# RWKV attention and ELU feed-forward on one core: a new written order for the first part of block 0

## The chip, the core and the metric

The kernel runs on one core of a Trainium2 chip. A core has five engines that matter here: PE (TensorE, matmuls and transposes by matmul), DVE (VectorE), ACT (ScalarE), POOL (GpSimd) and SP (SyncE, which here only issues loads). Each executes its own list of instructions in order, and they wait for each other by semaphores. The metric is the device time of one execution in microseconds (us).

## What is computed

```python
state = 0                                   # per batch b, head h: 48 x 48
for t in range(768):                        # B=4, H=8, S=768, D=48
    y[t]  = r[t] @ (state + outer(u * k[t], v[t]))
    state = w[:, None] * state + outer(k[t], v[t])
x = y as 3072 tokens x 384
h = x @ w_in                                # 384 -> 2048
g = where(h > 0, h, exp(min(h, 0)) - 1)
out = g @ w_out                             # 2048 -> 384
```

## The kernel before

The sequence is cut into six blocks of 128 tokens, and a block holds all four batches, so 4 x 128 = 512 tokens go through the feed-forward at once. A *unit* is one block of one batch: its r and k are turned by PE (`turn_in`, L628), multiplied by tables of powers of w (L688), multiplied with each other (`scores`, L768), masked, and applied to v (`first_outputs`, L880 and L824). The result is split in two halves of lower precision, xh (L899 on ACT) and xl (L901 on DVE). A *step* f of the feed-forward, 0 to 15, is one slice of 128 hidden columns: `hidden` (9 matmuls, L1031), `negative` (two on ACT, L1040 and L1041), `elu` (DVE, L1046), `split_g` (gh on ACT, L1052; gl on DVE, L1054), `project` (9 matmuls, L1075). `hidden(f)` uses the weights wh and wl of index f, part 1, and `project(f)` those of index f + 1, part 0.

In block 0 the weights arrive too. Load `Lw:j` brings w_in of f = j/2 for even j (four transfers, L212) and w_out of f = (j-1)/2 for odd j (one, L215) into six staging slots. Pair k is made of the loads 2k-1 and 2k: `wd:k` (`widen`, ACT, L571) reads both, `ma:k` (`merge`, DVE, L580) joins them, `sp:k` (`split_w`, POOL L591 and ACT L593) makes wh, and `rs:j` or `rsd:j` (`rest_w`, POOL L615 or DVE L615 and L617) makes wl, which frees the slot. `rsd:6` makes the part of wl that `hidden(3)` reads, called wl_131 in the order listings.

What stands when is written out by hand. `START` lists everything up to the first half of step 0, `BOTH` the steps 0 to 2 mixed with what block 1 needs early (`nT`: turning r and k of unit (1, 0), after `Lnk:0` loaded them; `ndr`, `ndk`: their tables). Steps 3 to 15 follow the line `FIRST`, later blocks `LATER`. Each name calls one function, and its instructions are put at the end of the lists of the engines that it uses. A name's variants differ in the engine:

```python
"kr": lambda b: self.key_rest(0, b),          # POOL, L740
"krd": lambda b: self.key_rest(0, b, dve),    # DVE
"m0": lambda b: self.mask_scores(0, b, 0),          # DVE
"m0a": lambda b: self.mask_scores(0, b, 0, True),   # ACT, then POOL
"S": lambda b: self.new_state(0, b),          # PE L924, then ACT L941
"Sd": lambda b: self.new_state(0, b, dve),    # PE L924, then DVE L941
```

Of the kernel before, what the change touches and what calls it, by code (L numbers as in the profile page):

```python
# [20 lines left out]
B, H, S, D = 4, 8, 768, 48  # L21
# [17 lines left out]
DEEP, WIDE = 3, 2  # L39

START = """
Lrk:2 Lv:1 Lrk:3 Lv:2 Lw:0 Lv:3 Lw:2 Lw:1 Lw:4 Lw:3 Lw:5
pr jk:8 inv rua:0 Tr:0 ub rub:0 Tk:0 dr:0 Tr:1 PT dk:0 A:0 dr:1 sum:0 rua:1 krd:0 zw m0:0 rub:1 Tk:1 vd:0 m1:0 ru:2
S:0 dk:1 Tk:2 Tr:2 A:1 ru:3 dr:2 dk:2 m0:1 sum:1 m1:1 Tr:3 dr:3 Tk:3 vd:1 dk:3 A:2 sum:2 Y:0 m0:2 wd:0 vd:2 A:3 m1a:3
sum:3 m0:3 xh:0 wdi:1 m1:2 Y:1 vd:3 ma:0 sp:0 wdo:1 xl:0 Y:2 xh:1 xh:2 rsd:0 mai:1 Lw:6 krd:3 spi:1 xl:1 mao:1 Y:3 H:0
"""
BOTH = """
xh:3 xl:2 xl:3 hid0 rsd:2 krd:2 wd:2 neg0 krd:1 spo:1 hid1 ma:2 elu0 sp:2 gh0 rs:1 Lnk:0 rs:3 neg1 Lw:8 gl0 Sd:1 rsd:4
wd:3 Sd:2 elu1 Lw:7 Lw:9 S:3 Lw:10 gh1 ma:3 proj0 sp:3 hid2 nT:0 gl1 nru:0 neg2 wd:4 proj1 rsd:6 Lnv:1 elu2 nsum:0 gh2
ma:4 ndr:0 ndk:0 Lnv:0 gl2 sp:4 rsd:5 Lw:12 wd:5 rsd:8 Lw:11 Lnk:1 rsd:7 nDp:0  # L50
"""
FIRST = """
Lq rk3 v3 Eq1 hid ns3 A1 T0 rud0 ma sum0 bkA-1 neg df0 elu sp dk0 pa1 brA-1 Y2 gh gl dr0 pb1 r4d xh2 xl2 mbT+1 mrT+1
# [1104 lines left out]
```

## Time and profile before

| | us |
|---|---|
| median of 3 runs | 497.84 (497.4 to 498.88) |
| the profiled execution | 498.67 |
| its span, first to last instruction | 496.9 |
| PE busy in the span | 485.8 (98%) |
| DVE, ACT, POOL busy | 304.7, 240.7, 106.5 |
| first `hidden` matmul starts at | 25.14 |
| `hidden(3)` starts at | 38.55 |

Times in the profile count from the start of the span. The profiled execution is 1.77 us longer than its span. A timeline row gives start, duration, engine, line, operation, names, size, and in brackets the idle time of the engine before it with what ended it; rows of the same kind in sequence are merged.

### The profile page before, as it was taken

The numbers are of one execution on the slowest core, as the hardware profiler recorded it, in microseconds if no ns is written. First come the engines' busy times: TensorE is split into PE (matmuls) and PEld (weight loads), VectorE is DVE, ScalarE is ACT, GpSimd is POOL, SyncE is SP. The second block draws the span as 40 slices with busy tenths as digits, with TensorE's granted clock in tenths as the row PEclk, the third lists the DMA queues.
The fourth block names the chain that finished last, engine by engine and source line by source line (L and its number), as shares of the span: only waits on it lengthen the run. The fifth ranks groups of instructions, "written<-read, shape, count | busy, mean of one in ns | idle before, by whom it ended". The sixth has DMA issues, their size and how long they took to land.

```text
span 496.9 us, 12118 instructions
## 1 busy us (share of the span) xinstructions
PE 485.8 (98%) x5013; PEld 403.2 (81%) x5013; DVE 304.7 (61%) x533; ACT 240.7 (48%) x458; POOL 106.5 (21%) x142
## 2 busy tenths in 40 slices
PE   8999999999999999999999999999999999999995
PEld 6787778787788888888888888888888878899995
DVE  7889998884676556657456575564674343433332
ACT  4278766744354444535435435445354354444442
POOL 7623332432132321221321321301011000000000
PEclk9999999999999999999999999999999999999999
DMA  8999986483454642544613625514443000011001
GB/s 136 225 215 201 211 203 195 83 166 92 111 96 119 134 113 41 139 113 72 125 49 86 150 67 110 138 44 91 108 80 90 11 1 2 8 33 24 1 0 69
DMA packets 108453, 49.11 MB, mean 99 GB/s; under 512 B 89442, under 2 KB 104292, under 8 KB 108388
## 3 DMA queue, kind: packets, MB, share of 16 engines
q1 hardware_dynamic: 96292, 43.52, 40.1%
q10 hardware_dynamic: 12096, 4.72, 3.9%
q8 instruction: 41, 0.67, 0.6%
q14 instruction: 24, 0.20, 0.1%
HBM read 35.12 MB, written 13.11 MB: 97 GB/s over the span
## 4 chain that ended last, share of the span: by engine, by line
PE 85%; DMA 6%; SPq 4%; DVE 2%; ACT 1%; issue 1%; DVEq 0%; ACTq 0%
PE ps_acc L1075 38%; PE ps_h L1031 36%; PE ps_a L792 4%; DMA stage<-in_moe_w_out_dram 3%; PE ps_y L824 3%; SPq L212 2%; PE ps_y L812 1%; DMA stage<-in_moe_w_in_dram 1%; PE ps_y L924 1%; SPq L169 1%; PE ps_y L807 1%; DMA r_t<-in_r_dram 1%; SPq L165 1%; ACT wide L571 1%; PE ps_a L768 0%
## 5 line engine op out<-in xcount | busy, mean ns | idle before, releaser
L1031 PE MATMUL ps_h<-x,wh 128*128 128x512 f32 (+1 forms) x582 | 193.9, 388 | 1.4 <-ACT x L899 1.3
L1075 PE MATMUL ps_acc<-g,wh 128*128 128x512 f32 x480 | 164.5, 397 | 0.1
L1046 DVE SCALAR_TENSOR_TENSOR ps_h<-g,ps_h 128x512 f32<-128x512 f32 x96 | 66.6, 694 | 129.9 <-ACT g L1041 129.8
L1031 PEld LDWEIGHTS ps_h<-x,wh 128*128 128x128 f32 x582 | 108.8, 188 | 24.2 <-ACT x L899 1.5
L1040 ACT ACTIVATE g<-ps_h 128x512 f32<-128x512 f32 x96 | 57.3, 597 | 128.6 <-PE ps_h L1031 102.5
L1031 PE MATMUL ps_h<-x,wl 128*128 128x512 f32 (+1 forms) x291 | 112.8, 388 | 0.0
L1075 PEld LDWEIGHTS ps_acc<-g,wh 128*128 128x128 f32 x480 | 90.1, 188 | 21.1 <-issue 0.8
L1075 PE MATMUL ps_acc<-g,wl 128*128 128x512 f32 x240 | 93.7, 390 | 0.0
L1054 DVE SCALAR_TENSOR_TENSOR g<-ps_h,g 128x512 fp32r<-128x512 f32 x96 | 66.3, 690 | 40.1 <-ACT g L1052 35.9
L1052 ACT ACTIVATE g<-ps_h 128x512 fp32r<-128x512 f32 x96 | 57.4, 598 | 67.8 <-DVE ps_h L1046 67.6
L1031 PEld LDWEIGHTS ps_h<-x,wl 128*128 128x128 f32 x291 | 54.6, 188 | 10.8
L1041 ACT ACTIVATE g<-g 128x512 f32<-128x512 f32 x96 | 60.7, 632 | 3.1
L842 POOL TENSOR_TENSOR a<-ident,diag 128x512 f32<-128x512 f32 x20 | 20.9, 1043 | 151.5 <-PE ps_y L924 88.9
L1075 PEld LDWEIGHTS ps_acc<-g,wl 128*128 128x128 f32 x240 | 45.1, 188 | 8.5
L676 POOL TENSOR_TENSOR tb<-rk,qw 128x512 f32<-128x512 f32 x16 | 20.7, 1294 | 69.9 <-DMA rk<-blocks 62.1
L1075 PE MATMUL ps_acc<-wh,g 128*128 128x384 f32 x128 | 35.2, 338 | 0.1
L849 DVE COPY_PREDICATED a<-mask,ps_a 128x512 f32<-128x512 int32 x40 | 29.3, 731 | 0.0
L838 ACT ACTIVATE a<-ident,diag 128x128 f32<-128x128 f32 x80 | 25.3, 392 | 0.0
L1075 PEld LDWEIGHTS ps_acc<-wh,g 128*128 128x128 f32 x128 | 23.4, 188 | 1.2 <-issue 0.5
L571 ACT ACTIVATE wide<-stage 128x768 f16<-128x768 bf16 (+1 forms) x18 | 17.8, 991 | 12.5 <-DMA stage<-in_moe_w_in_dram 10.6
L949 ACT CAST x<-ps_y 128x256 fp32r<-128x256 f32 (+1 forms) x40 | 10.8, 324 | 23.1 <-DVE state L939 21.6
L1075 PE MATMUL ps_acc<-wl,g 128*128 128x384 f32 x64 | 21.5, 336 | 0.0
(114 smaller groups left out, 438.5 us busy)
## 6 DMA issues: line engine op xcount, KB each, us to landing
blocks<-tb SPq DMA_DIRECT2D x64, 128.0 KB, 2.3
rk<-blocks SPq DMA_DIRECT2D x16, 512.0 KB, 3.5
stage<-in_moe_w_out_dram SPq DMA_DIRECT2D x16, 383.8 KB, 5.8
stage<-in_moe_w_in_dram SPq DMA_DIRECT2D x64, 95.8 KB, 4.5
out_dram<-stage ACTq DMA_DIRECT2D x80, 48.0 KB, 1.7
r_t<-in_r_dram SPq DMA_DIRECT2D x17, 192.0 KB, 4.3
k_t<-in_k_dram SPq DMA_DIRECT2D x17, 192.0 KB, 5.0
v_t<-in_v_dram SPq DMA_DIRECT2D x17, 192.0 KB, 5.3
```

Of the source, the lines that this page charges most:

```text
L571: self.nc.scalar.activation(top.rearrange("p s (f t) -> p s f t", t=2)[..., 1], self.place(self.late, k, DEEP, i).bitcast(BF16)[..., 2], A ...
L676: (self.nc.gpsimd if i else self.nc.vector).tensor_mul(dst, src, by)
L838: self.nc.scalar.activation(un["a"][i][:, a, :], self.ident, AF.Copy, scale=diag[:, a : a + 1])
L842: self.nc.gpsimd.tensor_mul(un["a"][i], self.ident.unsqueeze(1).to_broadcast([P, HP, P]), diag.unsqueeze(2).to_broadcast([P, HP, P]),)
L849: self.nc.vector.copy_predicated(un["a"][i], self.mask.bitcast(I32).unsqueeze(1).to_broadcast([P, HP, P]), un["pa"][i].rearrange("p (a t) ...
L1031: self.nc.tensor.matmul(ph[:, part], lhsT=a[:, c * P : (c + 1) * P], rhs=x[:, c, part], start=(c == 0 and i == 0), stop=(c == NC - 1 and i ...
L1040: nc.scalar.activation(g, ph, AF.Relu, scale=-1.0)
L1041: nc.scalar.activation(g, g, AF.Exp, scale=-1.0)
L1046: self.nc.vector.scalar_tensor_tensor(ph, g, -1.0, ph, op0=ALU.add, op1=ALU.max)
L1052: nc.scalar.activation(part, g, AF.Copy, scale=W_SCALE)
L1054: nc.vector.scalar_tensor_tensor(part, g, W_SCALE, self.g[n, f][2].bitcast(F32), op0=ALU.mult, op1=ALU.subtract)
L1075: self.nc.tensor.matmul(at, lhsT=lhs, rhs=rhs, start=(f == 0 and i == 0), stop=(f == NF - 1 and i == 2),)
```

## The change

Two of the four tables are written anew, `START` and `BOTH`; `FIRST`, `LATER` and all functions stay. The set of work is the same, and so is the work of each engine but for the entries whose variant changes: key_rest of all four units goes from DVE to POOL (`krd` to `kr`), rest_w 5 and 7 too (`rsd` to `rs`), `vd:0` from POOL to DVE, the first masked scores of unit 0 from DVE to ACT and POOL (`m0a:0`) and those of unit 3 the other way (`m1:3`), the state copies of units 2 and 3 change places between DVE and ACT.

```diff
 START = """
-Lrk:2 Lv:1 Lrk:3 Lv:2 Lw:0 Lv:3 Lw:2 Lw:1 Lw:4 Lw:3 Lw:5
-pr jk:8 inv rua:0 Tr:0 ub rub:0 Tk:0 dr:0 Tr:1 PT dk:0 A:0 dr:1 sum:0 rua:1 krd:0 zw m0:0 rub:1 Tk:1 vd:0 m1:0 ru:2
-S:0 dk:1 Tk:2 Tr:2 A:1 ru:3 dr:2 dk:2 m0:1 sum:1 m1:1 Tr:3 dr:3 Tk:3 vd:1 dk:3 A:2 sum:2 Y:0 m0:2 wd:0 vd:2 A:3 m1a:3
-sum:3 m0:3 xh:0 wdi:1 m1:2 Y:1 vd:3 ma:0 sp:0 wdo:1 xl:0 Y:2 xh:1 xh:2 rsd:0 mai:1 Lw:6 krd:3 spi:1 xl:1 mao:1 Y:3 H:0
+rua:0 ub Lrk:3 jk:8 Tr:0 rub:0 pr rua:1 rub:1 Tk:0 inv Lrk:2 Tr:1 dr:0 Tk:1 Lw:0 dk:0 A:0 dr:1 m0a:0 dk:1 sum:0 PT
+Lv:1 m1:0 Lv:2 Tr:3 vdd:0 A:1 sum:1 zw dr:3 Tk:3 m1:1 Tr:2 Tk:2 m0:1 dr:2 Y:0 Lv:3 wd:0 dk:2 A:2 dk:3 ma:0 Lw:1 Lw:2
+xh:0 ru:3 sum:3 xl:0 kr:0 sp:0 wdo:1 Lw:4 m0:2 S:0 Lw:3 ru:2 sum:2 vd:1 m1:2 vd:2 rsd:0 A:3 Y:1 xh:1 m0:3 wdi:1 m1:3
+Y:2 mao:1 xh:2 vd:3 xl:1 kr:1 Lw:6 mai:1 xl:2 Y:3 H:0 xh:3 xl:3 spi:1 rsd:2 Lw:5 wd:2
 """
 BOTH = """
-xh:3 xl:2 xl:3 hid0 rsd:2 krd:2 wd:2 neg0 krd:1 spo:1 hid1 ma:2 elu0 sp:2 gh0 rs:1 Lnk:0 rs:3 neg1 Lw:8 gl0 Sd:1 rsd:4
-wd:3 Sd:2 elu1 Lw:7 Lw:9 S:3 Lw:10 gh1 ma:3 proj0 sp:3 hid2 nT:0 gl1 nru:0 neg2 wd:4 proj1 rsd:6 Lnv:1 elu2 nsum:0 gh2
-ma:4 ndr:0 ndk:0 Lnv:0 gl2 sp:4 rsd:5 Lw:12 wd:5 rsd:8 Lw:11 Lnk:1 rsd:7 nDp:0
+Sd:1 hid0 neg0 ma:2 spo:1 kr:3 elu0 wd:3 gh0 Sd:3 Lnk:0 rs:1 hid1 sp:2 kr:2 neg1 gl0 ma:3 S:2 Lw:8 nT:0 rsd:4 Lw:7
+elu1 proj0 sp:3 Lnk:1 gh1 rs:5 Lw:11 Lw:10 hid2 nru:0 gl1 rs:3 proj1 nsum:0 nDp:0 wd:4 Lw:9 ma:4 neg2 sp:4 ndr:0 Lnv:0
+rs:7 elu2 rsd:8 gh2 ndk:0 wd:5 gl2 rsd:6 Lnv:1 Lw:12
 """
```

**First place: DVE, the end of `BOTH`.** These are DVE's instructions from `rsd:6` (the row that writes wl_131 by L617) to the last of step 2 in the kernel before; L1046 is `elu2`, L1054 is `gl2`, L580 is `ma:4`, the L688 rows are `ndr` and `ndk`.

```order
L617 SCALAR_TENSOR_TENSOR wl_131<-stage,wh_130 128x384
L1046 SCALAR_TENSOR_TENSOR ps_h<-g,ps_h 128x512
L733 TENSOR_REDUCE diag<-ru 128x8
L580 SCALAR_TENSOR_TENSOR stage<-stage,wide 128x768
L688 TENSOR_TENSOR rk<-ps_rT,pw 128x512
L688 TENSOR_TENSOR rk<-ps_kT,qw 128x512
L1054 SCALAR_TENSOR_TENSOR g_728<-ps_h,g_721 128x512
L615 TENSOR_TENSOR wl_131<-stage,wh_130 128x384
L617 SCALAR_TENSOR_TENSOR wl_133<-stage,wh_132 128x384
```

And DVE at the same place in the changed kernel, from `ma:4` on:

```order
L580 SCALAR_TENSOR_TENSOR stage<-stage,wide 128x768
L688 TENSOR_TENSOR rk<-ps_rT,pw 128x512
L1046 SCALAR_TENSOR_TENSOR ps_h<-g,ps_h 128x512
L617 SCALAR_TENSOR_TENSOR wl_133<-stage,wh_132 128x384
L688 TENSOR_TENSOR rk<-ps_kT,qw 128x512
L1054 SCALAR_TENSOR_TENSOR g_737<-ps_h,g_733 128x512
L617 SCALAR_TENSOR_TENSOR wl_131<-stage,wh_130 128x384
```

The L617 that writes wl_131 moved from ahead of `elu2` to behind `gl2`, and L617 of wl_133 (`rsd:8`) stands between `elu2` and `ndk`. On PE nothing changed there: `hidden(3)` follows `project(1)`, and its second matmul reads wl_131.

**Second place: PE, between `hidden(1)` and `project(0)`.** Before, after the last matmul of `hidden(1)`, come the products for the new states of units 1 to 3 (L924):

```order
L1031 MATMUL ps_h<-x,wh_126 128x512
L924 MATMUL ps_st<-v_t_73,k_t_72 32x48 x16
L924 MATMUL ps_st<-raw 32x48 x32
L1075 MATMUL ps_acc_664<-g_580,wh_126 128x512
L1075 MATMUL ps_acc_664<-g_580,wl_127 128x512
```

In the changed kernel, PE at the same place:

```order
L1031 MATMUL ps_h<-x,wh_126 128x512
L924 MATMUL ps_st<-raw 32x48 x16
L628 MATMUL ps_rT<-ident,r_t_68 128x128 x4
L628 MATMUL ps_kT<-ident,k_t_69 128x128 x4
L1075 MATMUL ps_acc_666<-g_587,wh_126 128x512
L1075 MATMUL ps_acc_666<-g_587,wl_127 128x512
```

One unit's states stay here (`S:2`), two moved ahead of `hidden(1)`, and the turning of unit (1, 0) (`nT`, L628), which stood behind `hidden(2)`, stands ahead of `project(0)`.

**Third place: ACT, step 1 to step 2.** Before, from `gh1` to `gh2`; the row L571 is `wd:4`, the rows L1040 and L1041 are `neg2`:

```order
L1052 ACTIVATE g_661<-ps_h 128x512
L593 ACTIVATE wh_130<-stage 128x384
L1040 ACTIVATE g<-ps_h 128x512
L1041 ACTIVATE g<-g 128x512
L571 ACTIVATE wide<-stage 128x768
L1052 ACTIVATE g_721<-ps_h 128x512
```

ACT in the changed kernel, from `gh1` to `gh2`:

```order
L1052 ACTIVATE g_682<-ps_h 128x512
L571 ACTIVATE wide<-stage 128x768
L1040 ACTIVATE g<-ps_h 128x512
L1041 ACTIVATE g<-g 128x512
L593 ACTIVATE wh_132<-stage 128x384
L1052 ACTIVATE g_733<-ps_h 128x512
```

`wd:4`, which needs the loads 7 and 8, moved from behind `neg2` to ahead of it. In the same way `wd:3` moved from behind `neg1` to ahead of `gh0`.

## Rows read from the trace of the kernel before

**Rows 1.** The page: busy time of PE, and the chain that ended last.

```profile
PE 485.8 (98%) x5013; PEld 403.2 (81%) x5013; DVE 304.7 (61%) x533; ACT 240.7 (48%) x458; POOL 106.5 (21%) x142
...
PE 85%; DMA 6%; SPq 4%; DVE 2%; ACT 1%; issue 1%; DVEq 0%; ACTq 0%
```

**Rows 2.** PE's waits: who ended them, us in total, times, longest.

```profile
PE ps_h L1031 <- ACT x L899: 1.3, 1, 1.3
PE ps_a L768 <- DVE rk L688: 0.6, 1, 0.6
```

**Rows 3.** PE's timeline from the first hidden matmul to step 3.

```profile
25.14 0.39 PE L1031 MATMUL ps_h<-x,wh 128*128 128x256 f32 x1 [1.27 <-ACT x L899]
...
30.21 0.55 PE L924 MATMUL ps_st<-v_t,k_t 128*32 128x48 f32 x32
...
31.40 0.50 PE L1075 MATMUL ps_acc<-g,wh 128*128 128x512 f32 x1
...
33.58 0.39 PE L1031 MATMUL ps_h<-x,wh 128*128 128x512 f32 x1
...
35.62 0.60 PE L628 MATMUL ps_rT<-ident,r_t 128*128 128x128 f32 x4
36.41 0.48 PE L1075 MATMUL ps_acc<-g,wh 128*128 128x512 f32 x1
...
38.77 0.39 PE L1031 MATMUL ps_h<-x,wl 128*128 128x512 f32 x1
```

**Rows 4.** ACT's timeline over the same steps.

```profile
24.13 0.63 ACT L571 ACTIVATE wide<-stage 128x384 f16<-128x384 bf16 x1 [0.78 <-DMA stage<-in_moe_w_out_dram]
...
35.82 0.60 ACT L1040 ACTIVATE g<-ps_h 128x512 f32<-128x512 f32 x1
36.45 0.63 ACT L1041 ACTIVATE g<-g 128x512 f32<-128x512 f32 x1
37.41 1.08 ACT L571 ACTIVATE wide<-stage 128x768 f16<-128x768 bf16 x1 [0.33 <-DMA stage<-in_moe_w_in_dram]
```

**Rows 5.** DVE's timeline: one merge beside POOL's work, then step 2.

```profile
20.18 1.20 DVE L580 SCALAR_TENSOR_TENSOR stage<-stage,wide 128x384 int32<-128x384 int32 x1
...
36.88 0.55 DVE L617 SCALAR_TENSOR_TENSOR wl<-stage,wh 128x384 fp32r<-128x384 f32 x1
37.35 0.69 DVE L1046 SCALAR_TENSOR_TENSOR ps_h<-g,ps_h 128x512 f32<-128x512 f32 x1
37.95 0.55 DVE L733 TENSOR_REDUCE diag<-ru 128x8 f32<-128x384 f32 x1
38.58 0.96 DVE L580 SCALAR_TENSOR_TENSOR stage<-stage,wide 128x768 int32<-128x768 int32 x1
39.45 0.68 DVE L688 TENSOR_TENSOR rk<-ps_rT,pw 128x512 f32<-128x512 f32 x1
40.05 0.68 DVE L688 TENSOR_TENSOR rk<-ps_kT,qw 128x512 f32<-128x512 f32 x1
40.65 0.68 DVE L1054 SCALAR_TENSOR_TENSOR g<-ps_h,g 128x512 fp32r<-128x512 f32 x1
41.25 0.55 DVE L615 TENSOR_TENSOR wl<-stage,wh 128x384 fp32r<-128x384 f32 x1
```

**Rows 6.** SP's timeline: the issue of the load of k for unit (1, 0).

```profile
27.34 0.53 SPq L165 DMA_DIRECT2D k_t<-in_k_dram  x1
```

**Rows 7.** The page, DMA issues: count, KB each, median us to landing.

```profile
k_t<-in_k_dram SPq DMA_DIRECT2D x17, 192.0 KB, 5.0
```

**Rows 8.** The chain that ended last, in order of time: start, us, what.

```profile
31.08 6.25 DMA stage<-in_moe_w_out_dram
```

**Rows 9.** Groups of POOL's instructions: busy us, mean ns of one, idle.

```profile
L740 POOL TENSOR_TENSOR k_t<-k_t,rev 128x384 f32<-128x384 f32 x8 | 8.2, 1024 | 0.0
```

**Rows 10.** Windows: length, busy us (instructions) by engine, granted clock, DMA share, GB/s.

```profile
24.00:26.00 2.00, 0.77 (x4) 0.57 (x5) 1.76 (x4) 1.87 (x5) 0.00 (x0) 1.00 1.00 303
```

## The prediction

> **What bounds the kernel now.** The page comes first: PE is busy 98% of the span, and 85% of the chain that ended last is PE [rows 1]. So a change is worth what it does to PE's idle time, and to nothing else as long as PE has work queued. PE's waits are few: the longest with work behind it is 1.3 us ahead of the first hidden matmul, the next is 0.6 us at the scores of a later step [rows 2]. PE's timeline tells where the first one stands: `hidden(0)` starts at 25.14 after 1.27 us of idling for xh, and from there PE goes through `hidden(1)`, the states (30.21), `project(0)` (31.40), `hidden(2)` (33.58), `nT` (35.62), `project(1)` (36.41) and `hidden(3)` with no gap that the timeline marks [rows 3]. The reason for the 1.27 us is on ACT: `wdo:1` waited for a load of w_out and ran at 24.13, and the xh of later units stood behind it [rows 4]. PE never idles around steps 1 to 3, but only since what it needs there is ready just before; the loads are not far ahead, as `wd:4` shows, which still waited 0.33 us for its load at 37.41 [rows 4]. All the changed entries lie before that point, so the whole effect is how much later or earlier PE reaches `hidden(3)`, and what later waits give back.
>
> **The start.** The turnings of all units come early, and ACT has the xh of unit 1 behind the load 1, which is now issued ahead of load 2. PE's own work up to `hidden(0)` is the same list in another order. Without the 1.27 us it would start at 25.14 - 1.27 = 23.87. The new order can add waits on the way (the turning of k of unit 1 is now asked for early), and I take 23.7 to 24.3, a gain of about 1.2 us here. Moving key_rest to POOL costs 1.02 us each there [rows 9] instead of 0.55 on DVE, and POOL's list is what the states now wait for; the DVE time it frees (4 x 0.5 us) lies under PE's work and is worth nothing by itself.
>
> **Between hidden(1) and project(0).** After 23.9, PE has the two halves of `hidden(0)`, two state products, `hidden(1)`, one more: 23.9 + (30.21 - 25.14) + 1.2 = 30.2 [rows 3]. It then stands before `nT`, 5 us earlier than before. The load of k was issued at 27.34 and lands 5.0 us later at the median of such loads, so at 32.3 [rows 6, 7]; ahead of it stand the same loads in either order, so I leave it there. Half of `nT` takes (36.41 - 35.62) / 2 = 0.4, so `project(0)` starts at 32.7 instead of 31.40. `gh0`, now behind `wd:3`, waits for the loads 5 and 6, which are issued ahead of that k, so I take it as no later. A second wait is inside this one: the state of unit 2 needs key_rest on POOL, which stands behind the wh of pair 2.
>
> So the 1.2 us are gone at this point, and 1.3 more are lost, less the 0.8 of `nT` that no longer follow `hidden(2)`. `project(0)` and `hidden(2)` take 35.62 - 31.40 = 4.22 [rows 3]; `hidden(2)` ends at 32.7 + 4.2 = 36.9, and `project(1)` starts at once, 0.5 us later than before.
>
> **The term that decides: rsd:6 behind gl2.** `hidden(3)` needs wl_131 from its second matmul on. Before, DVE made it at 36.88, ahead of `elu2` [rows 5], 1.3 us before PE asked at 38.77 [rows 3]. Now DVE makes it after `elu2`, `rsd:8`, `ndk` and `gl2`, so a spare item has become the end of a chain. From the end of `hidden(2)`: `neg2` on ACT 0.63 + 0.63 = 1.26 [rows 4]; then on DVE `elu2` 0.60 (37.35 to the next at 37.95), `rsd:8` 0.47 (36.88 to 37.35), `ndk` 0.60 (40.05 to 40.65), `gl2` 0.60 (40.65 to 41.25), `rsd:6` 0.55 [rows 5]; with 0.04 between the engines 4.12. PE has `project(1)` and one matmul in that time, 38.77 - 36.41 = 2.36 [rows 3]. So even if all else is on time, PE waits 4.12 - 2.36 = 1.76 us at `hidden(3)`.
>
> All else is not on time. `wd:4` now stands ahead of `neg2`, and it starts when its loads are there. Before, this was 37.41, the end of a transfer issued at 31.08 [rows 4, 8]; `neg2` would then start at 38.36 and `ma:4` on DVE end its turn at 39.45, `ndr` at 40.05 [rows 5], with `elu2` next. The remaining 0.60 + 0.47 + 0.60 + 0.60 + 0.55 = 2.82 put wl_131 at 42.87, which is 4.1 us after 38.77. Should the loads come early enough that `wd:4` is over by 36.9, the chain starts there and ends at 36.9 + 4.12 = 41.0, 2.3 us late. SP may run ahead, since it no longer waits for `rsd:0` late in the start, but the transfers in front are the same bytes; I take the middle, 3.2 us.
>
> One price the trace shows only in part: POOL's `rs:7` now runs beside `rsd:8`. A DVE merge that ran beside POOL's products took 1.20 us against 0.55 [rows 5], so up to 0.65 more may fall into the chain. The Trainium skill (SBUF — State Buffer, section SBUF: two separate sides) says that a DVE instruction with two SBUF inputs and a GpSimd instruction that reads SBUF exclude each other for a whole instruction, the loser standing still. By that rule the loss would be up to one rest_w on POOL. The row agrees in kind, 0.65 us in one case. I leave it out of the sum and put it into the upper end.
>
> **What comes back.** After step 3 PE has no slack of its own: a late PE makes `neg`, `elu` and the freeing of slots late too, so most of the 3.2 stays. The 0.6 us wait at later scores [rows 2] hangs on loads and may shrink; I give half of it back. Sum: +3.2 - 0.3 = +2.9. The profiled execution (span 496.9, total 498.67) would be 501.6, and 497.84, the median of the runs, becomes 500.7.
>
> **Rivals.**
> First, the lag is paid back by loads: if the DMA queue and not PE sets the pace of steps 4 to 9, the 0.6 us wait there vanishes whole, and the loads of pair 4 come at the early end. Then 2.3 - 0.6 = +1.7, 499.5. For it speaks `wd:4` waiting for a load [rows 4]; against it that PE's chain is 85% [rows 1] and that the loads wait for slots which the same late DVE frees.
>
> Second, not slower: the load of k and loads 7 and 8 land 2.5 us earlier than before, as SP's list has no stop in it. Then PE passes `nT` at 30.2 without waiting, `hidden(2)` ends near 35.2, wl_131 is there at 39.3, and the lag is 0.5, which later waits swallow: 497.8. The point from which it decides is the landing of k: at 30 or earlier this case holds, and at 32 mine. Against it speaks that the load had only been issued at 27.34 and that DMA was fully busy just before, share 1.00 at 24 to 26 [rows 10]. A real gain would need `rsd:6` not to bind, and 1.76 us of it are there whatever the loads do.
>
> Third, the clock. In all of the trace up to the end of PE's work the granted clock was 1.00 (2.4 GHz), also in the 2 us in which PE was busy for 0.77 [rows 10]. Now PE has two holes of some 2 us within 12 us. If the clock fell to its lower level, 1.2 GHz, `project` and `hidden` of one step (4.2 us) would take twice as long: +4.2, 504.6. The Trainium skill (TensorE: Matmul & The Clock Gate, Part 1) says that idle stretches of PE can bring the clock down until it is busy again. No wait in this trace was long enough to show it.
>
> **Chances.** The forecast, +2.0 to +4.5 (499.8 to 502.3): 0.60. The loads pay back, +0.7 to +2.0: 0.18. Not slower, -1.5 to +0.7: 0.12. The clock: 0.07. Faster by more than that, through something I don't see: 0.03. The range 498.4 to 502.6 leaves out the clock, the faster ends, and half of the second rival. A difference under 0.3% (1.5 us) can't be told from none here: faster 0.03, within it 0.19 (the second rival and some of the first), slower 0.78.
>
> **What would show it.** Right: `hidden(0)` starts near 24; PE waits at the k turning of `nT` (L628) for a DMA, 1 to 2 us, at about 31; PE waits at the second matmul of `hidden(3)` (L1031) for DVE L617, 1.8 to 4 us, and that matmul stands near 42 instead of 38.77; ACT's L571 ahead of `neg2` is ended by a DMA. Wrong: if no wait stands at `hidden(3)`, or if that wait is there but PE's steps near 75 stand where they stood, the lag having come back. A granted clock under 1.00 anywhere in 28 to 50 would be the third rival.

## The result and the profile after

| | before | after |
|---|---|---|
| median of five runs, same chip | 498.54 us (497.4 to 498.88) | 502.44 us (501.92 to 503.96) |
| the profiled execution, its span | 498.67, 496.9 | 501.92, 500.1 |
| ratio of the times, 95% interval | | 1.009, 1.0068 to 1.0112 |

The change makes the kernel slower. The profiled executions are 3.25 us apart, the medians 3.90, and the ratio, which takes all five runs of each, is worth 4.5 us (3.4 to 5.6) on 498.5. I had forecast +2.9. Three executions in the experiments below, whose mean clock was 0.85 or less (539, 604 and 806 us), are left out of the ratios.

The page of the kernel after, beside [rows 1]: PE does the same 5013 matmuls, and its busy time is 2.2 us longer, which is already a sign of slower matmuls somewhere.

```profile
PE 488.0 (98%) x5013; PEld 405.3 (81%) x5013; DVE 306.1 (61%) x528; ACT 240.6 (48%) x458; POOL 114.8 (23%) x147
...
PE 86%; DMA 3%; DVE 2%; ACT 1%; SPq 1%; issue 1%; POOL 1%; ACTq 0%; DVEq 0%
```

PE's waits after, beside [rows 2]: the wait for ACT's xh is gone, and a longer one for wl has come.

```profile
PE ps_h L1031 <- DVE wl L617: 2.6, 1, 2.6
...
PE ps_a L768 <- DVE rk L688: 1.3, 2, 0.7
```

PE's timeline after, first its start, then the steps that answer to [rows 3]:

```profile
5.06 1.61 PE L524 MATMUL ps_u<-rev 1*128 1x384 f32 x2 [0.17 <-DVE pw L139]
6.60 1.97 PE L520 MATMUL junk<-ident 128*128 128x128 f32 x8
8.36 1.06 PE L628 MATMUL ps_rT<-ident,r_t 128*128 128x128 f32 x4
...
10.68 0.60 PE L628 MATMUL ps_kT<-ident,k_t 128*128 128x128 f32 x4
...
25.72 0.39 PE L1031 MATMUL ps_h<-x,wh 128*128 128x256 f32 x1
...
31.60 0.55 PE L924 MATMUL ps_st<-raw 128*32 128x48 f32 x32
32.08 0.66 PE L628 MATMUL ps_rT<-ident,r_t 128*128 128x128 f32 x4
32.57 0.60 PE L628 MATMUL ps_kT<-ident,k_t 128*128 128x128 f32 x4
32.92 0.48 PE L1075 MATMUL ps_acc<-g,wh 128*128 128x512 f32 x1
...
35.06 0.39 PE L1031 MATMUL ps_h<-x,wh 128*128 128x512 f32 x1
...
37.10 0.39 PE L1075 MATMUL ps_acc<-g,wh 128*128 128x512 f32 x1
...
42.24 0.50 PE L1031 MATMUL ps_h<-x,wl 128*128 128x512 f32 x1 [2.64 <-DVE wl L617]
```

The second matmul of `hidden(3)` stands at 42.24 instead of 38.77, 3.47 us late, and the scores of a later step (L768, waiting 0.65 us as before) at 76.83 instead of 73.64, 3.19 late. The start reads oddly: until 10 us four turnings take 1.06 us, after that 0.60.

DVE's timeline after, beside [rows 5], and POOL's over the same time:

```profile
34.09 1.41 DVE L724 TENSOR_TENSOR ru<-r_t,k_t 128x384 f32<-128x384 f32 x1
35.53 1.27 DVE L728 TENSOR_TENSOR ru<-ru,u_b 128x384 f32<-128x384 f32 x1
...
37.79 0.94 DVE L580 SCALAR_TENSOR_TENSOR stage<-stage,wide 128x768 int32<-128x768 int32 x1
38.66 0.68 DVE L688 TENSOR_TENSOR rk<-ps_rT,pw 128x512 f32<-128x512 f32 x1
39.26 0.68 DVE L1046 SCALAR_TENSOR_TENSOR ps_h<-g,ps_h 128x512 f32<-128x512 f32 x1
39.85 0.67 DVE L617 SCALAR_TENSOR_TENSOR wl<-stage,wh 128x384 fp32r<-128x384 f32 x1
40.44 0.68 DVE L688 TENSOR_TENSOR rk<-ps_kT,qw 128x512 f32<-128x512 f32 x1
41.04 0.67 DVE L1054 SCALAR_TENSOR_TENSOR g<-ps_h,g 128x512 fp32r<-128x512 f32 x1
41.64 0.54 DVE L617 SCALAR_TENSOR_TENSOR wl<-stage,wh 128x384 fp32r<-128x384 f32 x1
```

```profile
34.04 2.35 POOL L615 TENSOR_TENSOR wl<-stage,wh 128x384 fp32r<-128x384 f32 x2
37.95 1.69 POOL L842 TENSOR_TENSOR a<-ident,diag 128x512 f32<-128x512 f32 x1 [1.55 <-DVE diag L733]
```

From 34 us on DVE never stands idle up to `rsd:6`, the last row. L724 and L728 take 1.41 and 1.27 here, beside POOL's `rs:5` and `rs:3` (L615). In the kernel before they took 0.55 and 0.56:

```profile
35.82 0.55 DVE L724 TENSOR_TENSOR ru<-r_t,k_t 128x384 f32<-128x384 f32 x1
36.40 0.56 DVE L728 TENSOR_TENSOR ru<-ru,u_b 128x384 f32<-128x384 f32 x1
```

ACT's `wd:4`, which waited for a load at 37.41 before [rows 4], has it early now:

```profile
34.84 1.09 ACT L571 ACTIVATE wide<-stage 128x768 f16<-128x768 bf16 x1
```

### The profile page after: what moved, and what is told of

Read it like the earlier page. It is cut to its first block, busy times and chain, and to the rows that moved or that the text cites. A ratio compares the mean times of both kernels' runs of the same rounds, so it can differ in the third digit from the quotient of the medians.

```text
span 500.1 us, 12117 instructions
## 1 busy us (share of the span) xinstructions
PE 488.0 (98%) x5013; PEld 405.3 (81%) x5013; DVE 306.1 (61%) x528; ACT 240.6 (48%) x458; POOL 114.8 (23%) x147
## 3 DMA queue, kind: packets, MB, share of 16 engines
q1 hardware_dynamic: 96292, 43.52, 38.6%
## 4 chain that ended last, share of the span: by engine, by line
PE 86%; DMA 3%; DVE 2%; ACT 1%; SPq 1%; issue 1%; POOL 1%; ACTq 0%; DVEq 0%
PE ps_acc L1075 39%; PE ps_h L1031 36%; PE ps_a L792 4%; PE ps_y L824 3%; DMA r_t<-in_r_dram 1%; PE ps_y L812 1%; PE ps_y L924 1%; DMA stage<-in_moe_w_in_dram 1%; PE ps_y L807 1%; SPq L212 1%; DMA stage<-in_moe_w_out_dram 1%; PE ps_a L768 1%; ACT wide L571 1%; DVE wl L617 1%; DVE stage L580 0%
## 5 line engine op out<-in xcount | busy, mean ns | idle before, releaser
L1046 DVE SCALAR_TENSOR_TENSOR ps_h<-g,ps_h 128x512 f32<-128x512 f32 x96 | 66.6, 693 | 131.9 <-ACT g L1041 131.7
L1040 ACT ACTIVATE g<-ps_h 128x512 f32<-128x512 f32 x96 | 57.3, 596 | 134.9 <-PE ps_h L1031 108.9
L1054 DVE SCALAR_TENSOR_TENSOR g<-ps_h,g 128x512 fp32r<-128x512 f32 x96 | 66.3, 690 | 39.5 <-ACT g L1052 35.2
L1041 ACT ACTIVATE g<-g 128x512 f32<-128x512 f32 x96 | 60.7, 632 | 3.1
L842 POOL TENSOR_TENSOR a<-ident,diag 128x512 f32<-128x512 f32 x20 | 21.5, 1076 | 151.5 <-PE ps_y L924 86.7
L591 POOL CAST wh<-stage 128x384 fp32r<-128x384 f32 x16 | 8.9, 554 | 47.7 <-DVE stage L580 47.7
```

Of the source, the lines that this page charges most:

```text
L842: self.nc.gpsimd.tensor_mul(un["a"][i], self.ident.unsqueeze(1).to_broadcast([P, HP, P]), diag.unsqueeze(2).to_broadcast([P, HP, P]),)
L1040: nc.scalar.activation(g, ph, AF.Relu, scale=-1.0)
L1041: nc.scalar.activation(g, g, AF.Exp, scale=-1.0)
L1046: self.nc.vector.scalar_tensor_tensor(ph, g, -1.0, ph, op0=ALU.add, op1=ALU.max)
L1054: nc.vector.scalar_tensor_tensor(part, g, W_SCALE, self.g[n, f][2].bitcast(F32), op0=ALU.mult, op1=ALU.subtract)
```

## Experiments

Theory A: the place of `rsd:6` makes the wait at `hidden(3)`. B: `ub` ahead of the warming matmuls keeps TensorE at its lower level at the start. C: POOL's work beside DVE's products of two SBUF tiles makes DVE late. The rival throughout: the loads set the pace. All times are ratios to runs of the kernel before on the same chip, the experiments in five rounds each. The last two columns are the places in PE's timeline of the scores of unit (1, 0) and of those near 74 us, in the profiled execution. That is one execution: in most of the slower kernels the ratio is worth more than the lag near 74 (with both back 2.7 us against 0.99), and where the difference arises is not settled.

| kernel | ratio, 95% interval | scores (1, 0) | near 74 |
|---|---|---|---|
| before | 1 | 40.79 | 73.64 |
| after | 1.009, 1.0068 to 1.0112 | 44.28 | 76.83 |
| after, rsd:6 back | 1.0059, 1.0036 to 1.0082 | 42.93 | 75.75 |
| after, ub back | 1.0109, 1.0081 to 1.0137 | 45.34 | 78.30 |
| after, both back | 1.0055, 1.0033 to 1.0076 | 41.88 | 74.63 |
| before, ub ahead | 1.0014, 0.9999 to 1.0029 | 40.87 | 73.64 |
| before, rsd:6 late | 1.0077, 1.0052 to 1.0101 | 44.60 | 77.51 |
| both back, rest_w 5 and 7 on DVE | 1.0082, 1.0063 to 1.0101 | 40.83 | 76.50 |
| new START, BOTH of before | 0.9984, 0.997 to 0.9998 | 39.43 | 73.15 |
| before, wdo:1 late | 0.9989, 0.9974 to 1.0005 | 40.43 | 73.18 |
| before, rest_w 5 on POOL | 1.0009, 0.9992 to 1.0026 | 41.22 | 73.94 |
| before, nT early | 1.0066, 1.0044 to 1.0088 | 42.85 | 75.71 |
| both back, nT late | 1.0049, 1.0032 to 1.0066 | 42.60 | 75.68 |
| new START, BOTH of before, vd of unit 1 on DVE | 1.0001, 0.9987 to 1.0015 | 40.55 | 73.81 |
| both back, nDp late | 1.0065, 1.0051 to 1.0079 | 42.47 | 76.00 |
| the same, nT late, gh0 first | 1.0077, 1.0062 to 1.0091 | 41.16 | 75.41 |

### rsd:6 and ub put back in the changed kernel

```diff
-... nDp:0 wd:4 Lw:9 ma:4 ... gl2 rsd:6 Lnv:1 Lw:12
+... nDp:0 wd:4 Lw:9 rsd:6 ma:4 ... gl2 Lnv:1 Lw:12
```

> The changed kernel with one entry put back: rsd:6 (DVE L617, writes wl_131) stands ahead of ma:4 instead of behind gl2. Theory A (the place of rsd:6 is the wait at hidden(3)): the 2.64 us wait of PE at L1031 for DVE L617 at 42.24 is gone, wl_131 is there by 38 and PE asks at 39.6; at most 0.3 us of wait is left there for other reasons, later waits stay as they are (0.65 at 76, 0.63 at 181), so the kernel is 2.0 to 2.6 us faster than the changed one: about +1.5 to +2.5 us over the kernel before in the median, span near 497.6. Rival (loads and slots pace steps 3 to 5, the place of rsd:6 only shows it): the wait moves to step 4 or 5, to wh or wl of the pairs 4 and 5 whose wd:5 waited 1.62 us for w_out at 42.24, and the kernel gains under 0.8 us.

```diff
-rua:0 ub Lrk:3 jk:8 Tr:0 rub:0
+rua:0 Lrk:3 jk:8 Tr:0 ub rub:0
```

> The changed kernel with one entry put back: ub (two one-row matmuls, L524) stands behind the first turning instead of ahead of the eight warming matmuls jk:8. Theory B (with ub ahead the run of warming matmuls is broken and TensorE stays at 1.2 GHz until about 10 us): the eight L520 take 1.06 us instead of 1.97, every group of four L628 takes 0.60 instead of 1.06, the first turning of r starts at about 5.8 instead of 8.36, hidden(0) near 24.5 instead of 25.72; the wait for k at about 32 and the wait at hidden(3) grow by most of that, so the time falls by 0 to 0.8 us only in the fastest runs, but the runs agree better (the changed kernel's runs spread over 2 us with mean granted clocks from 0.994 to 0.998; here all at 0.998 or 0.999). Rival (the slow rows at the start come from the loads' traffic, not from the clock): the rows stay at 1.06 and nothing changes.

Both edits:

> The changed kernel with both entries put back, rsd:6 ahead of ma:4 and ub behind the first turning. Theories A and B together: full clock from about 5 us, no wait at hidden(3), 2.4 to 3.4 us faster than the changed kernel; what is left over the kernel before is the wait for k ahead of project(0) and the slower POOL and DVE instructions, 0 to +1.5 us. Rival (loads pace): 0.8 us or less under the changed kernel.

With rsd:6 back the wait at `hidden(3)` is gone, as A says, and half of what it should free is not there: PE now waits at the scores, 1.44 us in the first run and 1.17 in the third, for the turned k (`ndk`), which stood behind the wait before. PE's timeline with both back:

```profile
41.88 1.16 PE L768 MATMUL ps_a<-rk 48*128 48x128 f32 x16 [1.17 <-DVE rk L688]
```

So it is DVE's list that is late, not one row of it. A's size falls: the ratio moves from 1.009 to 1.0059, about 1.5 us instead of 2.0 to 2.6 (the two intervals overlap; in the profiled executions it is 1.08 us near 74).

B's rows come as expected with ub back (eight L520 in 1.16 us, four turnings in 0.60), but the first run, with ub still ahead, had them too: 1.09 and 0.60. So ub ahead does not always bring the slow start. And the start is worth nothing here: with ub back `hidden(0)` starts at 24.41, and the second matmul of `hidden(3)` at 42.14 after 2.63 us of waiting, against 42.24 with `hidden(0)` at 25.72. What I had not expected came behind that wait. The windows of that run (length, busy us by engine, granted clock, DMA share, GB/s):

```profile
40.00:42.00 2.00, 0.00 (x0) 0.00 (x0) 2.00 (x4) 0.82 (x2) 1.22 (x2) 1.00 1.27 259
42.00:44.00 2.00, 1.86 (x6) 1.49 (x7) 1.04 (x2) 1.91 (x5) 0.10 (x1) 0.70 0.59 119
44.00:46.00 2.00, 2.00 (x10) 1.26 (x10) 0.00 (x0) 0.56 (x1) 1.44 (x2) 0.50 0.74 212
```

The granted clock falls to 0.50, 1.2 GHz. The same place in the profiled execution of the changed kernel, whose clock stayed at 1.00:

```profile
42.00:44.00 2.00, 1.76 (x8) 1.43 (x8) 0.77 (x2) 1.76 (x4) 0.00 (x0) 1.00 0.91 155
```

From the third matmul of `hidden(3)` to `project(2)` PE needs 4.35 us with ub back, first below, and 2.80 in the changed kernel, second:

```profile
42.48 0.79 PE L1031 MATMUL ps_h<-x,wh 128*128 128x512 f32 x2
...
46.83 0.50 PE L1075 MATMUL ps_acc<-g,wh 128*128 128x512 f32 x1
```

```profile
42.57 0.62 PE L1031 MATMUL ps_h<-x,wh 128*128 128x512 f32 x2
...
45.37 0.50 PE L1075 MATMUL ps_acc<-g,wh 128*128 128x512 f32 x1
```

So the fall costs 1.55 us. Of the six executions with ub back four had a mean granted clock of 0.994 or less, where I had expected 0.998 or more in all.

### ub alone, and rsd:6 alone, in the kernel before

```diff
-pr jk:8 inv rua:0 Tr:0 ub rub:0
+pr ub jk:8 inv rua:0 Tr:0 rub:0
```

> The kernel before with one entry moved: ub ahead of jk:8, all else as it was. Theory B: L520 x8 takes 1.8 to 2.0 us instead of 1.06, the turnings behind it take 1.06 per four instead of 0.60 until about 10 us, and the runs spread as those of the changed kernel do; since PE waited 1.27 us for xh ahead of hidden(0) at 25.14, half to all of the lag vanishes there: 0 to +1.5 us, mean granted clock below 0.999. Rival (the clock has to do with the other order of the changed kernel): rows at 1.06 and 0.60 as before, same time within 0.3 us.

The slow start is there (L520 x8 in 1.97 us, `hidden(0)` at 25.98 instead of 25.14), and at the scores only 0.08 us of it is left, none near 74. The ratio can't be told from 1. So ub ahead may be what gives the odd rows at the start of the changed kernel: turnings at 1.06 us come in two of three profiles with it and in none of the others. It explains none of the loss.

```diff
-... proj1 rsd:6 Lnv:1 elu2 ... Lnv:0 gl2 sp:4
+... proj1 Lnv:1 elu2 ... Lnv:0 gl2 rsd:6 sp:4
```

> The kernel before with one entry moved: rsd:6 (DVE L617, writes wl_131) stands behind gl2 instead of ahead of elu2, all else as it was. Theory A (its place alone makes PE wait at hidden(3)): DVE ends gl2 at 40.8 (all of step 2 moves up by the 0.47 that rsd:6 leaves), wl_131 is there at 41.3 instead of 37.4, PE's second matmul of hidden(3) starts at 41.3 to 41.5 instead of 38.77 after 2.5 to 2.8 us of waiting, and 2.2 to 2.8 of it are still there at the scores near 73.6; the time grows by 2.0 to 3.0 us. Rival (the wait in the changed kernel comes from DVE being late as a whole): the wait here is under 1.5 us and the time grows by less than 1.

This is the cleanest confirmation: one row of DVE moved, 2.51 us of waiting at `hidden(3)`, and a matmul there at 41.38, as worked out. PE, and the windows behind it:

```profile
41.38 0.50 PE L1031 MATMUL ps_h<-x,wl 128*128 128x512 f32 x1 [2.51 <-DVE wl L617]
41.72 0.82 PE L1031 MATMUL ps_h<-x,wh 128*128 128x512 f32 x2
...
42.76 1.06 PE L1031 MATMUL ps_h<-x,wh 128*128 128x512 f32 x2
```

```profile
42.00:44.00 2.00, 2.00 (x6) 1.59 (x5) 1.61 (x3) 0.00 (x0) 0.33 (x1) 0.50 0.51 154
```

Again the clock falls to 0.50, and two matmuls take 1.06 us instead of 0.62. The lag near 74 is 3.87 us, more than the wait, and the ratio 1.0077 is worth 3.8 us where 2 to 3 were expected. The one execution of this kernel with a mean clock of 0.999 took 500.84, 2.5 us above the mean of the kernel before, which is about the wait alone; but one at 0.993 took the same.

### POOL beside DVE

```diff
-... gh1 rs:5 Lw:11 Lw:10 hid2 nru:0 gl1 rs:3 ... rs:7 elu2 ... gl2 rsd:6 Lnv:1 Lw:12
+... gh1 Lw:10 hid2 rs:3 nru:0 gl1 ... rsd:6 ma:4 ... elu2 ... gl2 rsd:5 Lw:11 Lnv:1 Lw:12 rsd:7
```

> The changed kernel with rsd:6 ahead of ma:4 and ub behind the first turning (as the run that put both back), and with rest_w 5 and 7 on DVE behind gl2 instead of on POOL. Theory C (POOL's rest_w beside DVE's products of two SBUF tiles stretches both, and DVE's list sets when ndk is done): L728 takes 0.56 instead of 1.27, L724 at most 1.4, L617 of rsd:8 0.55 instead of 1.01, ndk is done 1 us or more earlier, the wait of 1.17 us at the scores (L768) near 41.9 falls to 0.3 or less, 0.8 to 1.2 us faster than with both put back. Rival (loads decide when ma:4 and ndk come): the rows get shorter, but the wait at the scores stays within 0.3 us of 1.17.

The rows come out as C says: L728 0.56 instead of 1.27, `rsd:8` 0.55 instead of 1.01, the scores at 40.83 with 0.54 us of waiting. One long row is left, `ma:4` (DVE), which starts while POOL's L842 is at work:

```profile
36.41 1.29 POOL L842 TENSOR_TENSOR a<-ident,diag 128x512 f32<-128x512 f32 x1 [2.15 <-DVE diag L733]
```

```profile
36.71 1.80 DVE L580 SCALAR_TENSOR_TENSOR stage<-stage,wide 128x768 int32<-128x768 int32 x1
```

In the changed kernel it was the other way round: L580 began at 37.79 and took 0.94, and L842, which began at 37.95, took 1.69. Who begins second pays. But the time did not fall (1.0082 against 1.0055 with both back; the expectation missed): slots are freed later, SP issues nothing from 36.7 to 41.9, and ACT's next `widen` waits 3.59 us for its load at 48.57. PE then waits 0.90 us at 53.94 (L628) and 1.87 at 60.55 (L768).

```diff
-... proj0 sp:3 hid2 ... gl2 sp:4 rsd:5 Lw:12
+... proj0 sp:3 rs:5 hid2 ... gl2 sp:4 Lw:12
```

> The kernel before with one entry changed: rest_w 5 on POOL behind sp:3 (rs:5) instead of on DVE behind gl2 (rsd:5), so that POOL's L615 stands beside nru (DVE L724, L728) as in the changed kernel. Theory C (a DVE product of two SBUF tiles and POOL's rest_w stretch each other): L724 takes 1.2 to 1.4 us instead of 0.55 or L728 1.0 to 1.3 instead of 0.56, POOL's L615 up to 1.5 instead of 1.03, DVE is 0.6 to 1.3 us late behind them; rsd:6 still ends by 38.7, as PE asks for it at 38.8, so the time stays within 0.3% (at most 0.5 us of wait at hidden(3) or at the scores). Rival (the long DVE rows of the changed kernel come from the loads' traffic at that time): L724 and L728 keep 0.55 and 0.56.

One rest_w of the kernel before on POOL, nothing else: DVE's L728 goes from 0.56 to 1.27, and POOL's L615 needs 1.27 instead of the 1.03 that the next one takes (at 44.23):

```profile
35.71 0.55 DVE L724 TENSOR_TENSOR ru<-r_t,k_t 128x384 f32<-128x384 f32 x1
36.30 1.27 DVE L728 TENSOR_TENSOR ru<-ru,u_b 128x384 f32<-128x384 f32 x1
```

```profile
35.88 1.27 POOL L615 TENSOR_TENSOR wl<-stage,wh 128x384 fp32r<-128x384 f32 x1
```

The 0.71 us become 0.59 us of waiting at the scores; the time moves by less than can be measured. C is shown for the rows and small by itself.

### Which half of the change loses, and nT

```diff
-Sd:1 hid0 neg0 ma:2 spo:1 kr:3 elu0 wd:3 gh0 Sd:3 ...
+hid0 krd:2 neg0 krd:3 spo:1 hid1 ma:2 elu0 sp:2 gh0 rs:1 Lnk:0 rs:3 ... (BOTH of before from here)
```

> START of the changed kernel (ub behind the first turning) with BOTH of the kernel before, less the five entries that START now holds, and with krd:3 in the place of krd:1. Theory (all that is lost is lost in BOTH; the new START by itself gains): hidden(0) starts at 24.1 to 24.5 instead of 25.14, no wait of PE over 0.4 us up to the scores of unit (1, 0), which start at 39.8 to 40.3 instead of 40.79; 0.5 to 1.0 us faster than the kernel before. Rival (the new START leaves DVE or the loads late and BOTH of before needs what they were): PE waits again for 0.8 us or more between hidden(0) and the scores, same time or slower than before.

`hidden(0)` is at 24.54, the scores at 39.43, 1.36 us early, more than expected; 0.87 of it is lost again by 74, to a wait of 0.64 us at 57.18 (L768 for DVE L688) above all. It ends slightly under the kernel before. So the new START alone loses nothing, and the loss comes with the new BOTH (which was not run behind the old START).

```diff
-sp:0 wdo:1 xl:0 Y:2 xh:1 xh:2 rsd:0
+sp:0 xl:0 Y:2 xh:1 xh:2 wdo:1 rsd:0
```

> The kernel before with one entry moved: wdo:1 (ACT L571, waits for a load of w_out until 24.13) stands behind xh:1 and xh:2 instead of ahead of them. Theory (the 1.27 us of PE's waiting ahead of hidden(0) is this ACT order alone and nothing behind it binds): hidden(0) starts at 23.9 to 24.2, PE's later steps up to 73 stand 0.8 to 1.2 us earlier, 0.8 to 1.2 us faster than before. Rival (something behind binds, wh of w_out for project(0) or the load of wd:4): the wait moves to L1075 of project(0) or to hidden(3), same time within 0.3 us.

The 1.27 us are gone: `hidden(0)` starts at 24.32 without a wait, 0.82 early, although this execution had a slow start (L520 x8 in 1.94 us, with the same list as the kernel before up to there). But its second half waits 0.38 us at 26.06 for the xh of the last unit (ACT L899), which now stands behind `wdo:1`, and 0.27 at 26.84 for xl (DVE L901). The scores are 0.36 us early and those near 74 0.46; in time it can't be told from before.

```diff
-... S:3 Lw:10 gh1 ma:3 proj0 sp:3 hid2 nT:0
+... S:3 Lw:10 nT:0 gh1 ma:3 proj0 sp:3 hid2
```

> The kernel before with one entry moved: nT:0 ahead of proj0 instead of behind hid2. Theory (PE waits for the load of k there, and what it loses stays): the load lands at 33.4 in that kernel, so PE waits about 1.6 us in all at L628 between 31.4 and 33.4, project(0) starts at 33.8 instead of 31.40, the scores of unit (1, 0) at 42.3 to 42.5 instead of 40.79, +1.5 to +1.8 us in the time, more where the clock falls in that wait. Rival (what is lost there is paid back by later waits, the 0.64 at the scores near 73 first): +0.8 us or less.

PE waits in two places around the turning, 0.86 and 0.72 us, and the lag stays: 2.06 us at the scores, 2.07 near 74. PE's timeline:

```profile
32.16 0.63 PE L628 MATMUL ps_rT<-ident,r_t 128*128 128x128 f32 x4 [0.86 <-PE ps_st L924]
33.50 0.63 PE L628 MATMUL ps_kT<-ident,k_t 128*128 128x128 f32 x4 [0.72 <-PE ps_rT L628]
```

PE is named as what ended these waits, but it had long been done. What ends 0.1 us ahead of each turning is a pair of DVE's state copies (L941), which read the product that PE put into PSUM just before:

```profile
31.34 0.71 DVE L941 COPY state<-ps_st 48x192 f32<-48x192 f32 x2
...
32.68 0.72 DVE L941 COPY state<-ps_st 48x192 f32<-48x192 f32 x2
```

In the code the states and the turnings take their PSUM (the memory that PE writes, in banks) from one ring of three banks at this point (tag "rw" in `bank`), so a turning right behind three states must wait until the copies have freed a bank. The size came as expected and the cause did not: it is a bank and not the load, so this run does not price the wait for k. The changed kernel avoids it, as two of the three states stand ahead of `hidden(1)` there.

With both back and nT moved back too:

> The changed kernel with rsd:6 ahead of ma:4, ub behind the first turning, and also nT:0 behind hid2 again. Theory C (DVE's list, made longer by POOL beside it, is what PE waits for at the scores): the 0.71 us of waiting for k goes, but ndk is not done earlier than 41.1, so the wait of 1.17 us at the scores grows to 1.6 to 2.0 and the scores start within 0.3 us of 41.88; same time within 0.5 us as with both put back. Rival (nT's place is the rest of the loss): the scores start at 41.2 or earlier, 0.7 us faster or more than with both put back.

The time is the same as with both back (1.0049 against 1.0055), and the scores don't come earlier, so the rival fails. The sizes are missed: the scores stand at 42.60, 0.72 us later and not within 0.3, after 1.43 us of waiting for `ndk` where 1.6 to 2.0 were expected. The wait at k went to `project(0)`, 0.58 us for `gh0`.

```diff
-ru:3 ... ru:2 sum:2 vd:1
+ru:3 ... ru:2 vdd:1 sum:2
```

> START of the changed kernel (ub behind the first turning) with BOTH of the kernel before as in the run of that name, and vd of unit 1 on DVE ahead of sum:2 (vdd:1) instead of on POOL. There PE waited 0.71 us at 19.80 for POOL L859, while DVE stood idle for 1.25 us up to 19.78. Theory (that wait is on the path to hidden(0) and nothing behind it binds): the wait falls to 0.3 us or less, hidden(0) starts at 24.0 to 24.2 instead of 24.54, the scores near 73 stand at 72.6 to 72.9, 0.3 to 0.6 us faster than without it, 0.8 to 1.3 faster than the kernel before. Rival (the next load binds): hidden(0) at 24.5 as before, no change.

A miss: the wait only fell to 0.51, a wait of 0.49 us that nothing in the profile ends came up at 23.80, `hidden(0)` starts at 25.02 and not 24.0 to 24.2, and no gain is left. This execution had a slow start too (L520 x8 in 1.88 us).

Two last runs asked whether POOL beside `ma:4` is what is left:

```diff
-... proj1 nsum:0 nDp:0 wd:4 ... sp:4 ndr:0 Lnv:0 rs:7 elu2 rsd:8 gh2 ndk:0 wd:5
+... proj1 nsum:0 wd:4 ... sp:4 ndr:0 Lnv:0 elu2 rsd:8 gh2 ndk:0 rs:7 nDp:0 wd:5
```

> The changed kernel with rsd:6 ahead of ma:4 and ub behind the first turning, and with nDp:0 (POOL L842) behind rs:7 at the end of step 2 instead of ahead of wd:4, so that POOL has nothing beside ma:4. Theory C (POOL beside DVE's products of two SBUF tiles makes DVE's list late, and PE waits for that list at the scores): ma:4 (L580) takes 0.95 us instead of 1.79, ndk ends 0.8 us earlier, the wait at the scores near 41.9 falls from 1.17 to 0.2 to 0.5 us, the lag at the scores near 74 from 0.98 to 0.1 to 0.4 us, 0.6 to 0.9 us faster than with both put back. Rival (ma:4 is long for another reason, such as the load of w_in): L580 keeps 1.5 us or more, no change.

> As the run before, with nT:0 behind hid2 again and gh0 ahead of wd:3 again. Theory: without POOL beside ma:4, DVE's list is no longer the last, so now nT's place counts: the 0.71 us wait for k is gone, project(0) starts at 30.8 to 31.2, the scores at 40.2 to 40.7 with under 0.4 us of waiting, 0.4 to 0.8 us faster than the run before; about the time of the kernel before (-0.5 to +0.3). Rival (loads and ma:3, later by wd:3, bind next): the wait moves to hidden(2) or project(1) (L1031 or L1075 for DVE L617), no gain over the run before.

`ma:4` takes 0.95 us and the wait at the scores halves to 0.58, near what C says, but the time does not follow. In the first run PE waited 1.43 us for POOL's key_rest of unit 2 at 31.52, as the loads for the pair ahead of it on POOL came late in that execution (`wd:2` waited 2.50 us for one). The run with ub back has a wait of 1.25 us at the same place, which the prediction had named as a second wait there. In the second nothing waits up to the scores but for 0.60 us there, which stand at 41.16; then 0.23, 0.63 and other waits follow, and near 74 the lag is 1.77. Which of the entries of BOTH makes steps 4 to 8 late there stays open.

## Why the prediction was right or wrong

**The start: too good, and without weight.** I forecast `hidden(0)` at 23.7 to 24.3. In the profiled execution it is 25.72, since TensorE was slow until 10 us; in the runs with that START (ub ahead or back) and a quick start it is 24.14 to 24.54. The gain I counted (1.2) is 0.6 to 1.0 where the start is quick, but it does not reach `hidden(3)`: 42.14 with 24.41, 42.24 with 25.72.

**Between hidden(1) and project(0): right number, another reason.** `project(0)` was forecast at 32.7 and came at 32.92. The load of k landed at 32.4, as forecast (32.3), but PE reached it only at 32.57, so the waiting for a DMA that I forecast isn't in this profile; PE was late itself, and the agreement is luck. In the run with both back it is there, 0.71 us (at 31.88, ended by the load of k). nT alone in the kernel before costs 2.07, but for a PSUM bank.

**The term that decides: right place, right sum, wrong parts.** The second matmul of `hidden(3)` was forecast near 42.0 and stands at 42.24, behind the wait for L617 that I named. The run that moves rsd:6 alone shows the mechanism by itself. But I had taken the middle of two ends because `wd:4` would wait for its load, and it did not: it ran at 34.84. So the early end should have held, `hidden(2)`'s end at 37.27 + 4.12 = 41.4. What filled the gap to 42.18 is POOL, which I had left out of the sum: `ma:4` and `ndr` were late by the 0.86 and 0.71 us that L724 and L728 were stretched, so `elu2` began at 39.26 instead of 38.6, and `rsd:8`, the one row that I had feared for, added 0.12. So the wait for the load was counted 0.9 us too high, POOL's stretching 0.8 too low and PE 0.4 too early, and the right sum is luck. The Trainium skill (SBUF — State Buffer, section SBUF: two separate sides) says that the one of the two that starts second is blocked until the first is through. L580 and L842 agree, in both orders (1.80 with 1.29, 0.94 with 1.69). In time the stretching was worth less than can be measured where it stood alone.

**What comes back: right number, another place.** 0.3 was forecast; 3.47 became 3.19 near 74. But the wait that I took it from is still 0.65 us there; what came back did so before 67. Later, at 181, PE waits 0.63 us at L924 for nothing that the profile names (the kernel before 0.47 at 131), and the lag ends at 3.2 in the span.

**The third rival: the step that failed, as far as the runs show it.** For the profiled pair, whose clock stayed at 1.00, the sum is near: +2.9 against +3.25. Over all runs it is short of +4.5 (3.4 to 5.6). The step that failed is that the sum took the clock as staying at 1.00 behind the wait: I gave its fall 7 in 100, and wanted two holes for it. One wait was enough in two of the three profiles that have it at `hidden(3)` (after 2.51 and 2.63 us of idling; not after 2.64): the clock fell to 0.50 right behind it. The price was wrong too: 1.55 us, where I had 4.2 (and 500.7 + 4.2 is 504.9, not 504.6). The Trainium skill (TensorE: Matmul & The Clock Gate, Part 1) says that idling brings the clock down. The trace agrees, by 0.50 in those windows.

So the term of 3.2 us is 3.2 or some 4.7, by execution. How often, in the changed kernel, is not shown. Of its five runs one had a mean granted clock of 0.994, the value of the profiled run with ub back, instead of 0.997 or 0.998, and it was the slowest, 503.96. It has no profile, and the kernel before, which has no such wait, had two runs at 0.993 as well (499.37 and 500.53). If one in five fell, that lifts the mean by 0.3 of the 1.6 us that are missing, and the profiled lag accounts for another 0.3. The cause of the rest, about 1 us, stays open. It lies in executions without a profile: the profiled one of the kernel before is 0.4 us above the mean of the five in the table, that of the changed kernel 0.8 below. Loads that land at other times are one candidate that was not tested.

**The first and second rival** did not hold as cases: no lag was paid back by loads, and k landed at 32.4, not before 30. But half of the second came true. The load that `wd:4` waited for before was issued at 30.21 and took 4.6 us to land, so at 34.8 instead of 37.3, the 2.5 us that it named. That did not help, since `rsd:6` still stood last on DVE, as the prediction says against this rival.

## What to carry to other kernels

An order in which one engine is nearly always busy has its slack in the rows that are ready early, so a row that PE will ask for must not go behind work of the same step, however short it is (moving one row of 0.5 us cost 3.8). When a change puts a wait of some 2.5 us on PE, count the clock too, and when a row goes from DVE to POOL look at what DVE does at that time: here DVE's products of two SBUF tiles collided with POOL's, and those with a PSUM operand didn't. And when a late list has several rows that are asked for, undoing one of them shows the next, so test the halves of a change before its rows.

## What the runs showed of the hardware

- The moment at which TensorE gets quick varies with one and the same list: eight L520 took 1.06 us in the kernel before and 1.94 in a run with the same list up to there; with ub ahead 1.97 twice and 1.09 once. The granted clock column shows 1.00 there in all of them, so it has to be read from the rows.
- POOL and DVE took turns by whole instructions where both read SBUF tiles: L728 0.56 alone and 1.27 beside one L615, which itself took 1.27 instead of 1.03. DVE's rows with a PSUM operand (L688, L1054, L1046) keep 0.68 beside POOL.
- A wait of 0.1 to 1.1 us at a group of L924 from 131 to 136 or from 178 to 184, put down to "issue", comes in 13 of the 16 profiles here, and its place moves with the order of the program; what it is was not found out.
